# Attention and FFN in fp32r pairs: the rounding remainders of the W2 chunks moved from GpSimd to VectorE

## The chip, the cores and the metric

The kernel runs on one core of a Trainium2 chip. Its time is the device time of one execution in microseconds (us). The engines are named as the profile names them: PE is TensorE, with PEld for its weight loads, DVE is VectorE, ACT is ScalarE, POOL is GpSimd, and SP is SyncE, which issues the DMAs. Each engine works through its own instructions strictly in the order in which the program lists them, and waits for other engines at semaphores.

## The reference

For 8 batches of 8 heads, 576 positions and 64 features per head, the reference computes two attentions, one over positions pooled by four and one over a band of seven neighbours, and adds them. The heads side by side make x of 8 x 576 x 512, on which a mixing block works:

```
out_d = softmax(q_d @ k_d.T / 8) @ v_d          # q_d, k_d, v_d: means over 4 positions
attn  = repeat(out_d, 4) + local_attn(q, k, v)  # |i - j| < 4
x     = heads of attn side by side              # [8, 576, 512]
u     = x + (x.T @ U @ V).T                     # U [576, 32], V [32, 576]
out   = u + relu(u @ w_ch1) @ w_ch2             # w_ch1 [512, 2048], w_ch2 [2048, 512]
```

U, V, w_ch1 and w_ch2 arrive in float64.

## The kernel before

A pair of heads is one unit of attention work: pair 4b + hp of batch b. Pairs 0 to 4 go through a version of the attention for the start of the kernel; the pairs from 5 on go through `late_global` (pooled attention), `local_attn` (band) and `mix_part` (U and V), which leave u of the pair as two tiles, uH (rounded to fp32r) and uL (the remainder). In `late_global` PE's `ps_a` matmuls (L552) give the pooled result, DVE scales it (`od`, L556), and SP stores it with four DMAs (L561). `mix_part` loads the pair's x from DRAM (`xL`, L822), splits it (ACT L839, POOL L840), multiplies by U on PE (`ps_hu`, L848, which needs the converted `Ust`) and by V (`ps_u`, L863), and ends in uH (ACT L869) and uL (POOL L871).

The FFN runs in 256 steps, (batch, half of 288 positions, one of 16 hidden chunks of 128). Step n of `ffn1` (F1 n, twelve matmuls at L888) uses W1 chunk n mod 16 and all four pairs' u of its batch; ACT (hH, L895) and DVE (hL, L896) turn its PSUM bank into two tiles; step n of `ffn2` (F2 n, twelve matmuls at L911) uses W2 chunk n mod 16. F1 33 is the first step of batch 1 and therefore the first that needs the u of pair 7.

Each weight matrix is held as a rounded part (H) and a remainder (L), since a product is taken as H·H + H·L + L·H. `convert` makes both from a raw float64 chunk: ACT takes the absolute value (L341), four DVE instructions build the float32 bits in the tile `cT` (L342, L344, L347, L349), ACT rounds them (L351, W2H), and POOL subtracts (L354, W2L). W1 and W2 come in 16 chunks of 128 x 512 each. Raw chunks wait in three buffers which they share with the product tiles `Pt` of the local attention (L799, L804). The tile `cT` also has three buffers.

No order is written by hand: every instruction is a `Plan.op` with a duration, a priority and its dependencies, and `Plan.run` plays a list schedule with those durations and emits every engine's instructions in the order that comes out. FFN steps have the lowest priority and fill PE. A changed duration or engine thus reorders all five engines from there on.

Of the kernel before, what the change touches and what calls it, by code (L numbers as in the profile page):

```python
# [11 lines left out]
F32 = mybir.dt.float32  # L12
# [4 lines left out]
ALU = mybir.AluOpType  # L17
# [36 lines left out]
class Plan:  # L54
# [6 lines left out]
    def buf(self, pool, shape, dt, name, tag=None, bufs=1):  # L61
        return Buf(self, pool, shape, dt, name, tag or name, bufs)

    def op(self, eng, dur, fn, r=(), w=(), prio=0.0, after=(), lat=None, move=0.0, at=0.0):
        o = Op()
        o.eng, o.dur, o.fn, o.prio, o.succ, o.ndep, o.ready = eng, dur, fn, prio, [], 0, at
        o.lat, o.move = LATENCY[eng] + SLACK * (SLACK_FROM <= prio < 1000) if lat is None else lat, move
        deps = set(after)
        bufs = []
        for k in r:  # L70
            b = k[0] if isinstance(k, tuple) else k
            bufs.append(b)
            if k in self.last_w:
                deps.add(self.last_w[k])
            self.readers.setdefault(k, []).append(o)
        for k in w:
            b = k[0] if isinstance(k, tuple) else k
            bufs.append(b)
            if k in self.last_w:
                deps.add(self.last_w[k])  # L80
            deps.update(self.readers.get(k, ()))
            self.readers[k] = []
            self.last_w[k] = o
        deps.discard(o)
        o.margin = MARGIN[eng] * (MARGIN_FROM <= prio < 1000 and any(d.eng != eng for d in deps))
        o.bufs = [b for b in dict.fromkeys(bufs) if isinstance(b, Buf)]
        for b in o.bufs:
            b.uses += 1
        for d in deps:
            d.succ.append(o)  # L90
        o.ndep = len(deps)
        self.ops.append(o)
        return o
# [108 lines left out]
def attn_mix_ffn_kernel(ctx: ExitStack, tc, q, kp, vp, qT, kT, v, U, Ub, V, w1, w2, mask, band, eye, pat, pool, vw, vn, ident, outT):  # L202
    nc = tc.nc
    B, H, S, D = q.shape
# [32 lines left out]
    op, buf = plan.op, plan.buf  # L237
# [24 lines left out]
    def dve(n, fn, r, w, prio, two_x=False):  # L262
        return op(DVE, ((n / 2 if two_x else n) + 65) / 960.0, fn, r, w, prio)

    def act(n, fn, r, w, prio, base=0.143):
        return op(ACT, n / 1200.0 + base, fn, r, w, prio)

    def pool_tt(n, fn, r, w, prio, ns=2.11, after=()):
        return op(POOL, 0.147 + n * ns / 1000.0, fn, r, w, prio, after)
# [10 lines left out]
    W2 = {}  # L280
# [39 lines left out]
    for _ in range(2):  # L320
        m = kept_tile([NS, 2, KW], "ms_b")
        op(POOL, 0.4, lambda m=m: nc.gpsimd.tensor_copy(
            out=m()[:, :, :, KL:KW].rearrange("p r h k -> p (r h) k"),
# [11 lines left out]
    def convert(raw, pp, n, hi_out, lo_out, a, wkey, name, prio, gate=(), l0=0):  # L335
        t = buf(ffn, [128, CN], I32, name, "cT:" + name, 3)
        w = lambda i: raw()[:pp, :2 * n].rearrange("p (n two) -> p n two", two=2)[:, :, i]
        ti = lambda: t()[:pp, :n]
        tf = lambda: t()[:pp, :n].bitcast(F32)
        ta = lambda: tf().rearrange("p (a n) -> p a n", a=a)  # L340
        act(n, lambda: nc.scalar.activation(tf(), w(1).bitcast(F32), AF.Abs), [raw], [t], prio)  # L341
        dve(1.6 * n, lambda: nc.vector.tensor_scalar(  # L342
            out=tf(), in0=tf(), scalar1=F_MIN, scalar2=F_MAX, op0=ALU.max, op1=ALU.min), [t], [t], prio, True)
        dve(1.6 * n, lambda: nc.vector.tensor_scalar(  # L344
            out=ti(), in0=ti(), scalar1=5, scalar2=2, op0=ALU.logical_shift_left,
            op1=ALU.logical_shift_right), [t], [t], prio, True)
        dve(1.2 * n, lambda: nc.vector.scalar_tensor_tensor(  # L347
            ti(), w(1), -0x40000000, ti(), op0=ALU.bitwise_and, op1=ALU.bitwise_or), [raw, t], [t], prio)
        dve(1.2 * n, lambda: nc.vector.scalar_tensor_tensor(  # L349
            ti(), w(0), 29, ti(), op0=ALU.logical_shift_right, op1=ALU.bitwise_or), [raw, t], [t], prio)  # L350
        act(n, lambda: nc.scalar.activation(hi_out(), ta(), AF.Copy), [t, *gate], [wkey + "H"], prio)  # L351
        if lo_out is None:
            return
        pool_tt(1.0 * n, lambda: nc.gpsimd.tensor_tensor(  # L354
            out=lo_out(), in0=ta()[l0:], in1=hi_out()[l0:].bitcast(F32), op=ALU.subtract),
            [t, wkey + "H"], [wkey + "L"], prio)

    def early_raw(name):
        return buf(early_pool, [128, S], I32, name, "eraw", 1)
# [4 lines left out]
    def load_ublk(prio):  # L364
        raw = early_raw("ur")
        dma(lambda raw=raw: nc.sync.dma_start(
            out=raw()[:, :2 * NS * R], in_=Ub.bitcast(I32)), [], [raw], prio, 164)
        convert(raw, 128, NS * R, lambda: Ublk[:, :, 0:R], None, NS, "Ub", "cu", prio)

    def load_u(prio):  # L370
        raw = raw_buf("ur")
        dma(lambda raw=raw: nc.sync.dma_start(out=raw()[:MP, :2 * MJ * R], in_=U.bitcast(I32)),
            [], [raw], prio, 150)
        convert(raw, MP, MJ * R, lambda: Ust[:, :, 0:R], lambda: Ust[:, :, R:2 * R], MJ, "U", "cu", prio)

    def load_v(prio):
        hs = S // 2
        for c in range(2):
            raw = early_raw("vraw")

            dma(lambda raw=raw, c=c: nc.sync.dma_start(
                out=raw()[:, :2 * hs], in_=V.bitcast(I32)[:, c * S:(c + 1) * S]), [], [raw], prio)
            cs = slice(c * hs, (c + 1) * hs)
            convert(raw, 128, hs, lambda cs=cs: Vst[:, cs].unsqueeze(1),
                    lambda cs=cs: Vst[3 * R:4 * R, cs].unsqueeze(1), 1, f"V{c}", "cv", prio, l0=3 * R)
# [590 lines left out]
    for i in range(len(steps) + LAG):  # L976
        if i < len(steps):
            b, t, fc = steps[i]
# [72 lines left out]
```

## Time and profile before

| | |
|---|---|
| Median of 3 runs (lowest, highest) | 1037.44 us (1034.21, 1039.74) |
| The profiled execution's own time | 1038.36 us |
| Its span | 1036.60 us |
| PE, PEld busy | 996.9 us, 975.3 us |
| DVE, ACT, POOL busy | 529.8 us, 388.0 us, 557.2 us |
| W2 chunks: first and last W2L instruction start | 100.7 us, 165.1 us |

The span is the stretch that the profiler recorded; the execution's own time has 1.76 us around it. Busy times of the whole span hide stages, so the rows further down are read stage by stage.

### The profile page before, as it was taken

The page shows a single profiled execution, that of the slowest core. Times are in us where ns is not written, and L with a number is a line of the kernel's source. Part 1 is how long each engine was busy: PE and PEld are TensorE (multiplying, and loading weights), DVE is VectorE, ACT ScalarE, POOL GpSimd, SP SyncE. Part 2 cuts the span into 40 slices and gives each one's busy share as a digit, 9 for nine tenths or more (in the row PEclk, how much of TensorE's full clock was granted, in tenths as well). Part 3 has the DMA queues.
Part 4 walks back from the last instruction along what each step waited for, and adds up shares of the span by engine and source line. Part 5 has one row for each costly group of instructions (what it writes and reads, how often), then busy time and mean ns, then how long its engine had stood idle before and what let it go on. Part 6 is the DMA issues. An engine that isn't in the chain of part 4 may idle for free.

```text
span 1036.6 us, 26946 instructions
## 1 busy us (share of the span) xinstructions
PE 996.9 (96%) x10831; PEld 975.3 (94%) x10831; DVE 529.8 (51%) x1054; ACT 388.0 (37%) x1234; POOL 557.2 (54%) x567
## 2 busy tenths in 40 slices
PE   6778898999999999999999999999999999999998
PEld 5667888999999999999999999999999999999998
DVE  5997898655554545444475344534652544211111
ACT  3676554442443434443344244423443232111110
POOL 4854568788575656565585638762765625211010
PEclk9896999999999999999999999999999999999999
DMA  8866764753555545545555355624644242000000
GB/s 279 226 172 179 199 186 116 149 138 104 135 137 115 141 113 132 128 86 146 120 137 125 87 132 133 143 75 101 151 116 117 64 113 50 24 1 24 1 24 23
DMA packets 222612, 120.30 MB, mean 116 GB/s; under 512 B 175492, under 2 KB 198456, under 8 KB 222488
## 3 DMA queue, kind: packets, MB, share of 16 engines
q1 hardware_dynamic: 222488, 118.58, 45.5%
q8 instruction: 85, 1.39, 0.6%
q14 instruction: 39, 0.32, 0.1%
HBM read 87.78 MB, written 30.75 MB: 114 GB/s over the span
## 4 chain that ended last, share of the span: by engine, by line
PE 84%; DVE 7%; POOL 3%; issue 2%; DMA 2%; ACT 2%; SPq 0%; DVEq 0%; POOLq 0%; ACTq 0%
PE acc L911 36%; PE ps_h L888 35%; PE ps_a L552 2%; PE ps_b L719 2%; DVE c L347 2%; PE ps_hu L848 1%; DVE c L349 1%; PE ps_t L539 1%; DMA w2r<-in_W 1%; PE ps_b L726 1%; POOL Pt L799 1%; DVE c L342 1%; DVE c L344 1%; PE ps_a L484 1%; PE ps_v L431 1%
## 5 line engine op out<-in xcount | busy, mean ns | idle before, releaser
L911 PE MATMUL acc<-hH,W2H 128*128 128x288 f32 x1024 | 310.5, 303 | 0.0
L896 DVE SCALAR_TENSOR_TENSOR hL<-ps_h,hH 128x288 fp32r<-128x288 f32 x256 | 116.6, 455 | 378.6 <-ACT hH L895 378.0
L888 PE MATMUL ps_h<-uH,W1H 128*128 128x288 f32 x1024 | 304.3, 297 | 4.1 <-DVE hL L896 3.1
L911 PE MATMUL acc<-hH,W2L 128*128 128x288 f32 x1024 | 303.1, 296 | 2.6 <-POOL W2L L354 2.6
L888 PE MATMUL ps_h<-uL,W1H 128*128 128x288 f32 x1024 | 303.4, 296 | 1.2 <-POOL uL L871 1.2
L911 PE MATMUL acc<-hL,W2H 128*128 128x288 f32 x1024 | 302.6, 296 | 0.0
L888 PE MATMUL ps_h<-uH,W1L 128*128 128x288 f32 x1024 | 302.0, 295 | 0.0
L799 POOL TENSOR_TENSOR Pt<-vl,at 128x896 f32<-128x896 f32 (+1 forms) x135 | 233.4, 1809 | 115.1 <-DVE acc L804 61.1
L895 ACT ACTIVATE hH<-ps_h 128x288 fp32r<-128x288 f32 x256 | 105.1, 410 | 433.6 <-PE ps_h L888 433.5
L888 PEld LDWEIGHTS ps_h<-uH,W1H 128*128 128x128 f32 x1024 | 193.5, 189 | 5.4 <-DVE hL L896 3.8
L911 PEld LDWEIGHTS acc<-hH,W2L 128*128 128x128 f32 x1024 | 193.2, 189 | 3.5 <-POOL W2L L354 3.5
L888 PEld LDWEIGHTS ps_h<-uL,W1H 128*128 128x128 f32 x1024 | 193.4, 189 | 1.5 <-POOL uL L871 1.5
L911 PEld LDWEIGHTS acc<-hH,W2H 128*128 128x128 f32 x1024 | 193.3, 189 | 1.1
L888 PEld LDWEIGHTS ps_h<-uH,W1L 128*128 128x128 f32 x1024 | 193.7, 189 | 0.0
L911 PEld LDWEIGHTS acc<-hL,W2H 128*128 128x128 f32 x1024 | 193.7, 189 | 0.0
L804 DVE TENSOR_REDUCE acc<-Pt 128x128 f32<-128x1024 f32 (+1 forms) x135 | 144.7, 1103 | 4.7 <-POOL Pt L799 2.3
L871 POOL TENSOR_TENSOR uL<-xT,uH 128x288 fp32r<-128x288 f32 x56 | 44.1, 811 | 71.3 <-ACT uH L869 71.2
L921 POOL TENSOR_TENSOR o<-uH,uL 128x288 f32<-128x288 f32 x64 | 49.8, 816 | 54.2 <-DMA out_t<-o 54.2
L840 POOL TENSOR_TENSOR xL<-xL,xH 116x640 fp32r<-116x640 f32 x28 | 44.0, 1572 | 64.2 <-ACT xH L839 49.3
L510 POOL TENSOR_TENSOR vr<-vr 72x256 f32<-72x256 f32 x54 | 42.4, 785 | 46.9 <-DMA vr<-in_v 46.8
L793 ACT ACTIVATE Pt<-ul 128x128 f32<-128x128 f32 (+1 forms) x135 | 48.4, 441 | 21.3 <-DVE acc L804 20.0
L744 ACT ACTIVATE se<-ps_b 96x114 f32<-96x114 f32 x108 | 38.5, 357 | 47.1 <-PE ps_b L719 34.1
(129 smaller groups left out, 1106.9 us busy)
## 6 DMA issues: line engine op xcount, KB each, us to landing
vl<-in_vp SPq DMA_DIRECT2D x54, 240.0 KB
out_t<-o SPq DMA_DIRECT2D x64, 144.0 KB
w1r<-in_W SPq DMA_DIRECT2D x16, 512.0 KB
w2r<-in_W SPq DMA_DIRECT2D x16, 512.0 KB
Y<-x_s SPq DMA_DIRECT2D x112, 72.0 KB
gT<-in_kT SPq DMA_DIRECT2D x27, 291.0 KB
xL<-x_s SPq DMA_DIRECT2D x28, 280.0 KB
gq<-in_qT SPq DMA_DIRECT2D x27, 288.0 KB
```

Source lines behind the costliest of these rows:

```text
L510: pool_tt(256, lambda x=x: nc.gpsimd.tensor_tensor(out=x()[:, :, 0:2, :], in0=x()[:, :, 0:2, :], in1=x()[:, :, 2:4, :], op=ALU.add), [x], ...
L744: act(n * KL, lambda p=ps[hh], se=se, n=n, rows=rows: nc.scalar.activation(se()[rows, 0:n].rearrange("p r k -> p (r k)"), p()[rows, 0:n * ...
L793: act(n * D, lambda n=n, ps=ps, Pt=Pt: nc.scalar.activation(Pt()[:, :n, :, 7], ul()[:, ps, :], AF.Copy), [ul], [(Pt, 1)], prio, 0.16)
L799: nc.gpsimd.tensor_tensor(out=Pt()[:, :n, :, 0:7].rearrange("p s d o -> p o s d"), in0=win, in1=at()[:, ps, :].rearrange("p s o -> p o s") ...
L804: dve(8.5 * n * D, lambda n=n, ps=ps, Pt=Pt: nc.vector.tensor_reduce(out=acc()[:, ps, :], in_=Pt()[:, :n], axis=AX.X, op=ALU.add), [(Pt, 0 ...
L840: pool_tt(640, lambda: nc.gpsimd.tensor_tensor(out=xL(), in0=xL().bitcast(F32), in1=xH().bitcast(F32), op=ALU.subtract), [xL, xH], [xL], prio)
L871: pool_tt(TN, lambda uH=uH, uL=uL, uf=uf: nc.gpsimd.tensor_tensor(out=uL()[:, hp, :], in0=uf(), in1=uH()[:, hp, :].bitcast(F32), op=ALU.su ...
L888: nc.tensor.matmul(ps()[:, :TN], w[:, dc, fs], u()[:, dc, :], start=(n == 0), stop=(n == 3 * NDC - 1))
L895: last_h[i] = act(TN, lambda: nc.scalar.activation(hH(), ps()[:, :TN], AF.Relu), [ps], [hH], FIRST, 0.05)
L896: dve(TN, lambda: nc.vector.scalar_tensor_tensor(hL(), ps()[:, :TN], 0.0, hH().bitcast(F32), op0=ALU.max, op1=ALU.subtract), [ps, hH], [hL ...
L911: nc.tensor.matmul(ac[e]()[:, :TN], W2[w][:, fc, es], hx(), start=(fc == 0 and n == 0), stop=(fc == NFC - 1 and n == 2))
L921: pool_tt(TN, lambda e=e, o1=o1: nc.gpsimd.tensor_tensor(out=o1()[:, :TN], in0=uH()[:, e, :].bitcast(F32), in1=uL()[:, e, :].bitcast(F32), ...
```

## The change

In `convert`, the subtraction for keys that begin with "W2" goes to DVE as a `tensor_tensor` of the same operands, planned with a length of 1.1 times the chunk; those of W1, U and V stay on POOL. Nothing else in the code changes, but the plan does, from the first W2 chunk on.

```
-        pool_tt(1.0 * n, lambda: nc.gpsimd.tensor_tensor(
-            out=lo_out(), in0=ta()[l0:], in1=hi_out()[l0:].bitcast(F32), op=ALU.subtract),
-            [t, wkey + "H"], [wkey + "L"], prio)
+        on = nc.vector if wkey[:2] == "W2" else nc.gpsimd
+        put = lambda: on.tensor_tensor(out=lo_out(), in0=ta()[l0:], in1=hi_out()[l0:].bitcast(F32), op=ALU.subtract)
+        (lambda *x: dve(1.1 * n, *x) if on is nc.vector else pool_tt(1.0 * n, *x))(
+            put, [t, wkey + "H"], [wkey + "L"], prio)
```

The new code has one line more, so behind `convert` its line numbers are one higher (the subtraction itself stands at L355).

On DVE, at the second and third W2 chunk (`c_1538`, `c_1591`; a number names one buffer of `cT`), there stands before:

```order
L347 SCALAR_TENSOR_TENSOR c_1538<-w2r,c_1538 128x512
L349 SCALAR_TENSOR_TENSOR c_1538<-w2r,c_1538 128x512
L342 TENSOR_SCALAR c_1591<-c_1591 128x512
L770 SCALAR_TENSOR_TENSOR ms<-sc,mask_sb 128x63
L344 TENSOR_SCALAR c_1591<-c_1591 128x512
L772 TENSOR_REDUCE lmx<-ms 128x9
L520 TENSOR_REDUCE mx<-ps_b 72x2
L347 SCALAR_TENSOR_TENSOR c_1591<-w2r,c_1591 128x512
```

and now:

```order
L347 SCALAR_TENSOR_TENSOR c_1538<-w2r,c_1538 128x512
L355 TENSOR_TENSOR W2L<-c_1528,W2H 128x512
L349 SCALAR_TENSOR_TENSOR c_1538<-w2r,c_1538 128x512
L342 TENSOR_SCALAR c_1591<-c_1591 128x512
L771 SCALAR_TENSOR_TENSOR ms<-sc,mask_sb 128x63
L521 TENSOR_REDUCE mx<-ps_b 72x2
L355 TENSOR_TENSOR W2L<-c_1538,W2H 128x512
L344 TENSOR_SCALAR c_1591<-c_1591 128x512
L897 SCALAR_TENSOR_TENSOR hL<-ps_h,hH 128x288
L347 SCALAR_TENSOR_TENSOR c_1591<-w2r,c_1591 128x512
```

Each chunk's subtraction stands one to five instructions behind the L349 of its own chunk, with pieces of the next chunk and of the attention between them; ACT's rounding has to happen in that gap. At the narrowest place (sixth chunk) only one short instruction and one L342 stand in it.

On PE, the first `ps_hu` matmuls that need `Ust` (pair 4) stand before between F1 18 and F2 16:

```order
L888 MATMUL ps_h_2562<-uL_838,W1H_88 128x288
L888 MATMUL ps_h_2562<-uH_832,W1L_89 128x288
L848 MATMUL ps_hu_2598<-xH_1705,Ust_86 64x128 x5
L848 MATMUL ps_hu_2598<-xL_1557,Ust_86 64x128 x5
L911 MATMUL acc0_1652<-hH_2497,W2H_1567 128x288
```

and now between F1 21 and F2 17:

```order
L889 MATMUL ps_h_2643<-uL_838,W1H_88 128x288
L889 MATMUL ps_h_2643<-uH_832,W1L_89 128x288
L849 MATMUL ps_hu_2666<-xH_1689,Ust_86 64x128 x5
L849 MATMUL ps_hu_2666<-xL_1557,Ust_86 64x128 x5
L912 MATMUL acc0_2687<-hH_2493,W2H_1567 128x288
```

Between the same attention work, 48 FFN matmuls (F1 19, 20 and 21, and F2 16) have come to stand ahead of them.

Further on in PE's order, the `ps_a` matmuls of pair 9 stand before within F2 27, behind F1 29:

```order
L911 MATMUL acc2_2693<-hH_3166,W2L_1568 128x288
L552 MATMUL ps_a_3295<-vs_3034,E_2905 72x64 x4
L552 MATMUL ps_a_3295<-vs_3268,E_2920 72x64 x4
L863 MATMUL ps_u_3310<-Vst_87,stk_3275 128x288
L911 MATMUL acc3_2699<-hH_3166,W2H_1567 128x288
```

and now within F2 28, behind F1 30:

```order
L912 MATMUL acc2_2724<-hH_3195,W2L_1568 128x288
L553 MATMUL ps_a_3335<-vs_2832,E_2934 72x64 x4
L553 MATMUL ps_a_3335<-vs_3289,E_2975 72x64 x4
L912 MATMUL acc3_2703<-hH_3195,W2H_1567 128x288
```

They have moved back by 26 matmuls: one F1, one F2 and the two `ps_u` of pair 6, which both stood behind them before.

On SP, the load of the last W2 chunk stood ahead of the four `od` stores of pair 7 and of the score stores of pair 8; it now stands behind the four `od` stores and the first four of the eight score stores. The `od` stores of pair 9 stand, as before, directly ahead of the load of `xL` of pair 7. On POOL the sixteen W2L instructions are gone, and the first three `Pt` products come closer together.

## Rows read from the trace of the kernel before

**Rows 1.** The page: the span, the engines' busy times, PE's 40 slices in tenths.

```profile
span 1036.6 us, 26946 instructions
...
PE 996.9 (96%) x10831; PEld 975.3 (94%) x10831; DVE 529.8 (51%) x1054; ACT 388.0 (37%) x1234; POOL 557.2 (54%) x567
...
PE   6778898999999999999999999999999999999998
```

**Rows 2.** Busy us by stretch: PE, PEld, DVE, ACT, POOL; granted clock, DMA share, GB/s.

```profile
100.00:125.00 25.00, 22.81 (x251) 21.75 (x250) 21.32 (x39) 13.77 (x38) 12.36 (x10) 0.93 0.82 213
125.00:150.00 25.00, 23.24 (x259) 21.93 (x260) 22.82 (x40) 13.65 (x37) 16.40 (x18) 0.93 0.64 190
150.00:175.00 25.00, 20.51 (x233) 19.57 (x232) 23.89 (x41) 12.59 (x41) 20.60 (x16) 0.93 0.43 111
...
128.00:132.00 4.00, 4.00 (x109) 3.55 (x109) 3.97 (x12) 1.60 (x4) 1.18 (x2) 0.63 0.21 42
...
168.00:172.00 4.00, 3.98 (x24) 3.98 (x25) 3.32 (x11) 1.88 (x10) 4.00 (x5) 0.57 0.35 103
```

**Rows 3.** Waits of PE from 96 to 205 us: total, times, longest.

```profile
PE acc L911 <- POOL W2L L354: 2.6, 4, 1.0
PE ps_hu L848 <- POOL Ust L354: 2.5, 1, 2.5
PE ps_h L888 <- DVE hL L896: 2.3, 2, 1.4
PE ps_a L552 <- POOL vs L512: 0.5, 1, 0.5
PE ps_t L539 <- ACT E L525: 0.5, 1, 0.5
```

**Rows 4.** Timeline of DVE (start, duration, instruction), from 96 us on.

```profile
101.26 1.65 DVE L349 SCALAR_TENSOR_TENSOR c<-w2r,c 128x512 int32<-128x512 int32 x1
...
111.31 0.68 DVE L349 SCALAR_TENSOR_TENSOR c<-w2r,c 128x512 int32<-128x512 int32 x1
111.91 0.42 DVE L342 TENSOR_SCALAR c<-c 128x512 f32<-128x512 f32 x1
...
156.90 4.02 DVE L342 TENSOR_SCALAR c<-c 128x512 f32<-128x512 f32 x1
```

**Rows 5.** Timeline of POOL at the first and at the last of those DVE instructions.

```profile
100.70 1.66 POOL L354 TENSOR_TENSOR W2L<-c,W2H 128x512 fp32r<-128x512 f32 x1 [2.53 <-ACT W2H L351]
...
159.35 1.28 POOL L354 TENSOR_TENSOR W2L<-c,W2H 128x512 fp32r<-128x512 f32 x1
```

**Rows 6.** The tile W2L on POOL: durations in ns (least, median, most), first and last start.

```profile
L354 POOL TENSOR_TENSOR W2L<-c,W2H x16: 1263/1312/3420, 100.7 to 165.1; 128x512 fp32r<-128x512 f32 x16
```

**Rows 7.** Timeline of ACT at the fourth and the sixth W2 chunk.

```profile
112.03 0.63 ACT L351 ACTIVATE W2H<-c 128x512 fp32r<-128x512 f32 x1 [1.40 <-DVE c L349]
...
119.88 0.67 ACT L341 ACTIVATE c<-w2r 128x512 f32<-128x512 f32 x1 [3.62 <-DMA w2r<-in_W]
120.45 0.62 ACT L351 ACTIVATE W2H<-c 128x512 fp32r<-128x512 f32 x1
```

**Rows 8.** Timeline of PE: pair 9's `ps_a`, F1 30, pair 7's `ps_hu`, F1 33.

```profile
211.83 1.19 PE L552 MATMUL ps_a<-vs,E 72*72 72x64 f32 x16
...
213.45 0.29 PE L888 MATMUL ps_h<-uH,W1H 128*128 128x288 f32 x1
...
215.04 0.29 PE L863 MATMUL ps_u<-Vst,stk 128*128 128x288 f32 x1
...
226.01 0.47 PE L848 MATMUL ps_hu<-xH,Ust 116*64 116x128 f32 x5
...
232.06 0.40 PE L888 MATMUL ps_h<-uL,W1H 128*128 128x288 f32 x1 [1.23 <-POOL uL L871]
```

**Rows 9.** Timeline of SP's queue: pair 9's `od` stores, pair 7's `xL` load.

```profile
213.51 3.74 SPq L561 DMA_DIRECT2D up_s<-od  x4
217.36 0.47 SPq L822 DMA_DIRECT2D xL<-x_s  x1
```

## The prediction

> **What bounds the kernel now.** I read the page first. PE is busy for 996.9 of 1036.6 us, and its slices are full from the eighth on; before that they are at 5 to 8 tenths [rows 1]. So the time is PE's work plus what PE idles or runs slowly in the first 235 us, and a change that only touches DVE and POOL can move the time only through that. The windows then show where: from 100 to 175 us PE is busy for 22.81, 23.24 and 20.51 of 25 us, while DVE is the fullest of the other engines (21.32, 22.82, 23.89) [rows 2]. The W2 conversion lies just there, its sixteen subtractions on POOL starting between 100.7 and 165.1 us [rows 6]. The list of PE's waits says what ended the idle time: W2L 2.6, Ust 2.5, hL 2.3, and 0.5 twice for attention work, together 8.4 us [rows 3]. The granted clock adds to it: it stands at 0.63 from 128 to 132 us and at 0.57 from 168 to 172, where the 2.5 us wait for Ust has just ended [rows 2, 3]. These are stretches mixed from the two levels of 1.2 and 2.4 GHz, and they cost (1 - 0.63) x 4 = 1.5 and (1 - 0.57) x 4 = 1.7 us. So 8.4 + 3.2 = 11.6 us is all that this stage can give back.
>
> A second place decides whether it is given back. F1 33 needs the u of pair 7 and waits for POOL's uL until 232.06 us [rows 8]. Followed back, that chain goes over `ps_hu` of pair 7 at 226.01 to the load of its `xL` at 217.36, which SP could issue only behind the `od` stores of pair 9 (213.51, 3.74 us), and those need pair 9's `ps_a` on PE at 211.83 [rows 8, 9]. From `ps_a` to F1 33 it is 20.2 us, of which PE's place in its own order sets the start. Behind F1 33 the slices are full again. The end thus moves by as much as pair 9's `ps_a` moves.
>
> **What the change removes.** DVE's timeline shows an effect of POOL that the groups hide. L349 on a 128x512 chunk lasts 0.68 us at 111.31, but 1.65 at 101.26, and POOL runs a W2L from 100.70 until 102.36: DVE's instruction ends 0.55 us after POOL's, as if it had begun there [rows 4, 5]. Fourteen DVE instructions from 101.26 to 161 us overlap a W2L in this way. Their excess over the clear duration, counted only until the W2L ends (0.98 us for the first; for the last, the 4.02 us L342 at 156.90, the 1.1 us of the W2L at 159.35 in which no other POOL instruction ran), adds up to 13.0 us. This goes.
>
> **What it adds.** Sixteen subtractions of 128x512 with two operands from SBUF. The nearest row is L349, of the same shape and also with two tensors read: L342 starts 0.60 us behind it (111.31 to 111.91) [rows 4]. 16 x 0.60 = 9.6 us of DVE time. The Trainium skill, "VectorE: DVE Perf Modes", section "The TRN2 errata", gives a float32 tensor_tensor (N + 151) / 0.96 ns, an estimate of 0.69 us here and 11.1 us for sixteen; by it the DVE sum would be 1.5 us worse.
>
> The new subtraction can wait in two ways. It needs ACT's rounding, which needs L349: at its best ACT takes 0.63 us [rows 7] and starts at once, and the DVE work put between (one to five instructions) mostly covers that. Five of sixteen roundings came late, by 3.6 us in all, as at 120.45, where ACT stood at the load of the next chunk until 119.88 [rows 7]. I take 2 us. What stands behind it on DVE is the next chunk and an hL, and for hL PE waits. And it can meet POOL's other work: POOL is busy for 49.4 us of these 75, of which some 16 x 1.31 = 21 are W2L [rows 2, 6], so it is met a third of the time, for about half a POOL instruction, 0.45 us: 16 x 0.34 x 0.45 = 2.4 us. DVE's balance is -13.0 + 9.6 + 2 + 2.4 = +1.0; without either wait it is -3.4, with waits of a whole W2L's length (0.98) each it is +12.3. So DVE is not relieved by much and the W2 chunks come about when they came. POOL saves 21 us here, which no wait of PE asks for: it waited for ACT.
>
> **What it moves.** (1) 48 FFN matmuls now stand ahead of the first `ps_hu`. At 1.59 us for twelve (F1 30 from 213.45 to the next instruction at 215.04) [rows 8] that is 6.4 us of cover, so the 2.5 us wait for Ust goes and, with the gap, the 1.7 us of slow clock behind it: 4.2 us. F2 16 among them now needs the last W2L, whose load comes later on SP, behind stores that PE's attention work releases; I take the last chunk to be ready at about 166 us, as before (165.1 + 1.3) [rows 6]. (2) Of the waits for W2L and hL, 4.9 us, I take back 3: a chunk's remainder takes 0.6 us on DVE where it took 1.3 and more on POOL, but hL shares DVE with it. The 1.0 us for attention work and the slow clock at 128 us stay. Recovered: 7.2 of 11.6 us; the ends are 0 and 11.6. (3) Pair 9's `ps_a` stands 26 matmuls later: 26 x 1.59 / 12 = 3.4 us more work ahead of it. With all F2 steps of batch 0 now done before pair 7's `ps_hu`, less FFN work covers the way to F1 33, but the way itself is no longer.
>
> **The sum.** +3.4 - 7.2 = -3.8 us. Against the profiled execution's 1038.36 that is 1034.6; this execution lies 0.9 above the median of 1037.44, so for the median 1033.6. The ends of the recovered time give 1037.44 + 3.4 = 1040.8 and 1037.44 + 3.4 - 11.6 = 1029.2.
>
> **The rivals.** What a measurement of this kernel can tell from no change is about 0.5%, 5.2 us, so 1032.3 and 1042.6 are the borders.
> - *PE gets nearly all of it back.* If neither wait of the new subtraction is there, DVE saves 3.4 us, the chunks come ahead of PE, and 9 to 11.6 us are recovered: 1029 to 1032 for the median. For it: only one gap on DVE is shorter than ACT's rounding. Against it: DMA is at 0.82 and 0.64 of its share in the first two windows [rows 2], and ACT waited for raw chunks, so the pace of the loads may hold. 0.3.
> - *The subtraction meets POOL in full: slower.* If each of the sixteen waits about as long as L349 did behind a W2L, DVE ends the stage 12.3 us later instead of 1.0; F2 16 and all behind it start 11 us later than in the forecast, and the time is 1045. It crosses the border at 9 us instead of 11, an average wait of (10 + 13.0 - 9.6) / 16 = 0.84 us. For it: in the 4.02 us row one DVE instruction let several of POOL's pass, and three `Pt` products now stand close together near the last chunks. Against it: the long POOL instructions of this stage were the W2L themselves. The Trainium skill, "SBUF — State Buffer", section "Who interferes with whom", speaks for it: a DVE instruction with two SBUF inputs and a GpSimd instruction that reads SBUF exclude each other, and the second to issue waits in full. By that rule the move changes who waits but doesn't end the conflict. The trace agrees with the waiting (0.98 us); how often it is met no run shows yet. 0.10.
> - *Nothing changes.* What PE gets back by 170 us it stands still for at F1 33, since the loads and stores of pairs 5 to 7 set that time and not PE's order: 1037. For it: PE had 1.23 us of waiting there already [rows 8]. Against it: the chain's start is on PE. It lies within the borders, as the forecast does: 0.6 together, of which 0.45 for the forecast.
>
> Chances: faster 0.3, same 0.6, slower 0.1. The range from 1029 to 1041 holds the forecast, the unchanged case and most of the gain; it leaves out the slower rival and the deepest gain.
>
> **What would show each step.** Right: L347 and L349 on w2r mostly at 0.68 us, with few above 1.3; the W2L group on DVE has a mean of 0.7 to 0.9 us; no wait of PE for Ust, and a clock of 1.00 behind 168 us; pair 9's `ps_a` near 209 us and F1 33 near 229 us; the rest of the slices full as before. Wrong: a W2L group on DVE of more than 1.2 us, or DVE idle for ACT's W2H by more than 4 us in all; PE waits for W2L or hL above 5 us in sum; a wait at F1 33 of more than 4 us, by which PE's gain would be lost again; or PE gaps behind 240 us, which before had none and which would mean that the new order starves a later batch.

## The result, and the profile of the changed kernel

| | before | the change |
|---|---|---|
| Median, 20 runs each (lowest, highest) | 1038.32 us (1034.21, 1042.65) | 1041.99 us (1038.79, 1046.42) |
| Ratio to before, 95% interval | | 1.0037 [1.0025, 1.0050] |
| The profiled execution, its span | 1038.36, 1036.6 us [rows 1] | 1040.94, 1039.2 us |

The forecast was 1033.6 us, 3.8 faster; the change is 3.7 us slower, just above the forecast range of 1029 to 1041. The page of the changed kernel (span, busy times, PE's slices in tenths) shows PE's work unchanged and POOL relieved of 23 us:

```profile
span 1039.2 us, 26944 instructions
...
PE 994.1 (96%) x10831; PEld 972.6 (94%) x10831; DVE 531.2 (51%) x1070; ACT 387.1 (37%) x1234; POOL 534.2 (51%) x551
...
PE   6778898999999999999999999999999999999998
```

To compare stages I use one measure throughout: **PE's loss** in a stretch is the time in which it was not busy plus (1 - granted clock) x length of the stretch. The clock has two digits, so the value of one window is good to some 0.3 us. The windows of the kernel before (columns as in [rows 2]):

```profile
100.00:150.00 50.00, 46.05 (x510) 43.68 (x510) 44.14 (x79) 27.42 (x74) 28.76 (x27) 0.93 0.73 202
150.00:200.00 50.00, 45.51 (x524) 44.32 (x523) 38.97 (x69) 23.76 (x77) 38.04 (x33) 0.97 0.52 130
200.00:260.00 60.00, 58.00 (x608) 57.09 (x608) 34.16 (x64) 20.93 (x64) 50.70 (x47) 1.00 0.52 125
```

and of the changed one:

```profile
100.00:150.00 50.00, 42.44 (x490) 39.98 (x489) 41.60 (x86) 26.17 (x73) 12.85 (x16) 0.97 0.73 193
150.00:200.00 50.00, 45.53 (x534) 44.29 (x534) 40.34 (x79) 24.88 (x79) 29.53 (x26) 1.00 0.51 126
200.00:260.00 60.00, 57.48 (x541) 56.96 (x541) 36.34 (x65) 20.28 (x64) 51.09 (x47) 0.97 0.58 139
```

From 100 to 200 us, before: 3.95 + 3.5 + 4.49 + 1.5 = 13.4; now: 7.56 + 1.5 + 4.47 + 0 = 13.5. The W2 stage gave back nothing in this profile. From 200 to 260 us it is 2.0 before and 2.52 + 1.8 = 4.3 now. What ended PE's idle time from 96 to 205 us, and then from 205 to 260 us:

```profile
PE ps_h L889 <- DVE hL L897: 7.4, 6, 2.3
PE acc L912 <- ACT W2H L351: 2.3, 1, 2.3
PE acc L912 <- DVE W2L L355: 1.4, 2, 0.7
PE ps_a L553 <- ACT E L544: 0.8, 1, 0.8
PE ps_b L727 <- DVE od L557: 0.8, 1, 0.8
...
PE ps_u L864 <- DVE stk L854: 1.7, 1, 1.7
PE ps_hu L849 <- POOL xL L841: 0.8, 1, 0.8
```

The wait for Ust (2.5 us in [rows 3]) is gone and W2L has fallen from 2.6 to 1.4, but hL has risen from 2.3 to 7.4 and W2H has come with 2.3. The second place is new: PE stands at pair 7's `ps_hu` and `ps_u` instead of at F1 33 [rows 8]. The subtraction itself behaves as forecast (its tile on DVE; durations least, median, most):

```profile
L355 DVE TENSOR_TENSOR W2L<-c,W2H x16: 671/680/1123, 102.3 to 169.6; 128x512 fp32r<-128x512 f32 x16
```

### The profile page after: what moved, and what is told of

Same layout as the page of the kernel before. It is cut to its first block, busy times and chain, and to the rows that moved or that the text cites. A ratio compares the mean times of both kernels' runs of the same rounds, so it can differ in the third digit from the quotient of the medians.

```text
span 1039.2 us, 26944 instructions
## 1 busy us (share of the span) xinstructions
PE 994.1 (96%) x10831; PEld 972.6 (94%) x10831; DVE 531.2 (51%) x1070; ACT 387.1 (37%) x1234; POOL 534.2 (51%) x551
## 4 chain that ended last, share of the span: by engine, by line
PE 86%; DVE 5%; DMA 4%; ACT 2%; issue 1%; SPq 0%; DVEq 0%; ACTq 0%
PE acc L912 37%; PE ps_h L889 37%; PE ps_a L553 2%; DMA w2r<-in_W 2%; PE ps_b L720 2%; PE ps_hu L849 2%; PE ps_t L540 1%; PE ps_b L727 1%; PE ps_a L485 1%; DVE c L347 1%; PE ps_u L864 1%; DVE c L349 1%; PE ps_v L432 1%; DMA s_s<-se 1%; DVE c L342 0%
## 5 line engine op out<-in xcount | busy, mean ns | idle before, releaser
L805 DVE TENSOR_REDUCE acc<-Pt 128x128 f32<-128x1024 f32 (+1 forms) x135 | 144.7, 1103 | 6.2 <-ACT Pt L794 2.9
L745 ACT ACTIVATE se<-ps_b 96x114 f32<-96x114 f32 x108 | 38.4, 356 | 51.3 <-PE ps_b L720 38.4
```

The costliest lines, as they stand in the source:

```text
L745: act(n * KL, lambda p=ps[hh], se=se, n=n, rows=rows: nc.scalar.activation(se()[rows, 0:n].rearrange("p r k -> p (r k)"), p()[rows, 0:n * ...
L805: dve(8.5 * n * D, lambda n=n, ps=ps, Pt=Pt: nc.vector.tensor_reduce(out=acc()[:, ps, :], in_=Pt()[:, :n], axis=AX.X, op=ALU.add), [(Pt, 0 ...
```

## The experiments

Every kernel was compared with the kernel before on the same chip; the kernel before had medians of 1038.1 to 1039.3 us there, so the ratios compare, not the medians. The change ran 20 times, the others 6 to 12 times. All results, with PE's loss worked out as above from each one's own windows:

| kernel | median us | ratio [95%] | loss 100-200 | loss 200-260 |
|---|---|---|---|---|
| before (two profiles) | | | 13.4, 13.9 | 2.0, 2.6 |
| the change (two profiles) | 1041.99 | 1.0037 [1.0025, 1.0050] | 13.5, 12.7 | 4.3, 4.8 |
| e1: old order, DVE | 1037.62 | 0.9983 [0.9970, 0.9995] | 11.7 | 2.1 |
| e2: new order, POOL | 1046.98 | 1.0083 [1.0064, 1.0102] | 19.2 | 3.8 |
| e3: old order, none | 1036.51 | 0.9976 [0.9957, 0.9995] | 8.9 | 2.9 |
| e4: new order, none | 1041.12 | 1.0011 [0.9995, 1.0027] | 12.8 | 4.4 |
| e5: change, W2 loads up | 1041.55 | 1.0039 [1.0019, 1.0059] | 10.2 | 8.0 |
| e6: old order, pair 9 later | 1041.93 | 1.0028 [1.0012, 1.0044] | 14.1 | 4.7 |
| e7: change, another plan | 1044.88 | 1.0059 [1.0039, 1.0079] | 15.3 | 3.8 |
| e8: e1, W2 loads up | 1040.18 | 1.0023 [1.0005, 1.0041] | 12.9 | 2.6 |
| e9: change, pair 7 loads up | 1043.81 | 1.0045 [1.0024, 1.0066] | 14.7 | 3.4 |
| e10: e1, pair 7 loads up | 1038.12 | 1.0001 [0.9981, 1.0022] | 12.3 | 2.6 |
| e11: e5, pair 7 loads up | 1041.79 | 1.0028 [1.0013, 1.0043] | 11.5 | 7.1 |
| e12: e9, pair 7 chain up | 1042.84 | 1.0050 [1.0036, 1.0065] | 15.0 | 5.6 |
| e13: e11, pair 7 chain up (two profiles) | 1043.65 | 1.0054 [1.0041, 1.0067] | 10.9, 10.7 | 5.4, 5.6 |
| e14: e10, pair 7 chain up | 1038.99 | 1.0006 [0.9990, 1.0022] | 11.7 | 4.8 |

### The engine and the order apart (e1 to e4)

The change does two things: another engine subtracts, and the plan lists everything in another order. e1 keeps the old plan and issues the subtraction on DVE; e2 keeps the new plan and issues it on POOL; e3 and e4 leave the subtraction out under either plan, and their matmuls read W2H where they would read W2L, so their output is not the reference's.

```
e1, against before:
-        pool_tt(1.0 * n, lambda: nc.gpsimd.tensor_tensor(
+        on = nc.vector if wkey[:2] == "W2" else nc.gpsimd
+        pool_tt(1.0 * n, lambda: on.tensor_tensor(
e2, against the change:
-        put = lambda: on.tensor_tensor(...)
+        put = lambda: nc.gpsimd.tensor_tensor(...)
e3 and e4, against before and the change (where wkey[:2] == "W2", planned but nothing issued):
...
-                for n, (w, hx) in enumerate((("H", hH), ("H", hL), ("L", hH))):
+                for n, (w, hx) in enumerate((("H", hH), ("H", hL), ("H", hH))):
```

> The plan still counts the W2 subtractions as POOL's, so PE, ACT and SP have exactly the order of before; only the sixteen instructions are emitted on DVE, where the plan's start times put them. Order theory (the loss is the new order: pair 9's ps_a 26 matmuls later, the last W2 load behind score stores): no loss here, 3 to 6 us faster than before, since the 13 us of DVE stalls behind W2L go and 9.6 us come. Engine theory (sixteen subtractions in DVE's line, waiting for ACT, delay hL and W2L whatever the order): 3 to 5 us slower than before, as the change.

> The plan counts the W2 subtractions as DVE's, so PE, ACT and SP have exactly the order of the change; the sixteen instructions are emitted on POOL. Order theory: slower than before by 3 us or more, like the change, or worse by the stalls that POOL's W2L bring back. Engine theory: within 1 us of before.

> Order of before with the sixteen W2 subtractions left out and the matmuls that read W2L reading W2H instead (same number and shape). The bound of what the subtraction costs on either engine in this order. Order theory: about as e1 or 1 to 3 us better, so 4 to 9 us faster than before. Engine theory: 4 us or more faster than e1.

> Order of the change with the sixteen W2 subtractions left out, W2H read in place of W2L. Order theory: still not faster than before (1037 to 1042), since loads and the places on PE stay. Engine theory: 4 us or more faster than the change, so at or below before.

Read the ratios by columns. New against old order costs 0.0054 with DVE (5.6 us), 0.0083 with POOL (8.6 us; before itself is the old order) and 0.0035 with nothing (3.6 us). DVE in place of POOL gains 1.8 us in the old order and 4.8 in the new one. So the engine is not what makes the change slower; the order is, and it does so even where there is no subtraction at all. The order theory has the direction in all four, but not the size: e1 was to gain 3 to 6 us and e3 4 to 9. e3 is also the ceiling of what the engine can give: without any W2 subtraction the old order gains 2.5 us (interval 0.5 to 4.5), and e1 has 1.8 of them.

PE's waits say the same. In the eight profiles of the old order, with the subtraction on POOL, on DVE or left out, PE waits 1.6 to 2.6 us for Ust and 1.5 to 3.5 for hL from 96 to 205 us. In the ten profiles of the change's order (e7 has another) it never waits for Ust, and 4.7 to 7.9 us for hL; e4, without any subtraction, has the 4.7.

Why POOL is so much dearer in the new order has one visible part. In e2 PE waits 4.9 us for one hL, which stands on DVE behind a short instruction on U's chunk that lasts 3.38 us (0.23 in the change) while POOL runs three instructions one after another, the last of them a W2L that ends at 172.59. From the timelines of PE and DVE in e2:

```profile
174.24 0.61 PE L889 MATMUL ps_h<-uH,W1H 128*128 128x288 f32 x1 [4.92 <-DVE hL L897]
...
169.31 3.38 DVE L344 TENSOR_SCALAR cu<-cu 116x160 int32<-116x160 int32 x1
```

### Pair 9 moved alone (e6)

Pair 9's `ps_a`, `od` and stores, and pair 7's loads behind them, stand 24 FFN matmuls and two `ps_u` later in the old order.

```
...
+        nxt = [x for x in ffn if at[x] > at[group[0]]]
+        order = [x for x in order if x not in self.late]
+        i = order.index(nxt[LATER - 1]) + 1
+        order[i:i] = group
```

> The kernel before, with one thing moved: pair 9's ps_a, its od multiplication and store, and pair 7's xL and Y loads behind them stand 24 FFN matmuls and two ps_u later, about where the change has them. If the chain ps_a, od, store, xL load, ps_hu sets the start of F1 33, as the prediction's step (3) has it, TensorE waits 4 to 5 us more for xL or uL ahead of F1 33 and the kernel takes 3 to 4 us more than before: 1041 to 1043 us. If the chain has slack, the wait grows by under 1 us and the time is that of before within 1 us: 1038 to 1040 us, and the change's 4 us come from the W2 stage alone.

It costs 2.9 us, interval 1.2 to 4.6, and the loss from 200 to 260 us rises from 2.0 and 2.6 to 4.7. The waits grow less than expected: uL from 1.2 to 2.1 us, and 1.8 us in four short ones ahead of it (1.0 for xL). The forecast's term of +3.4 us for this move holds in size.

### The W2 loads ahead of the score stores (e5, e8)

In the change the last W2 load is issued at 158.81 us (150.62 before), behind `od` stores and the first score stores, and ACT waits 14.8 us for these loads instead of 9.0. Both kernels list each W2 load directly behind the last use of the buffer that it fills.

```
...
+                to = max([first[held[k - 1]]] + [last[b] for b in held[:k - 2]]) + 1
+                if to < at[o]:
+                    order.remove(o)
+                    order.insert(to, o)
```

> The change with one thing altered: on the SP queue the six later W2 loads stand directly behind the last use of the buffer that they replace, ahead of the score stores that they stood behind; every other engine's order is the change's. Theory L (the late W2 loads set the pace of the W2 stage: the last load was issued 8.2 us later than before and ACT waited 14.8 us for loads): 2 to 4 us faster than the change, 1038 to 1040 us, with ACT's waits for the W2 loads under 9 us, the last W2L before 168 us and TensorE's waits for hL behind 164 us under 2.5 us. Theory D (VectorE's own line, in which hL stands behind the softmax work of the next pair, sets the pace): as the change, within 1 us (1041 to 1043), TensorE's hL waits stay above 4 us. Theory S (the stores that are pushed back cost as much as the loads gain): within 1 us too, but with waits for the score tiles' buffers in place of those for hL.

> The order of the kernel before, with the W2 subtraction on VectorE and the six W2 loads ahead of the score stores on SP. Theory L: 1 to 3 us faster than before, 1035 to 1037 us, and at least 0.5 us faster than the same order without the loads moved (ratio below 0.997 to before). Theory D or S: the same as without the loads moved, ratio 0.997 to 1.000 to before.

In e5 ACT's wait for the loads falls to 8.9 us, the first `ps_hu` comes at 173.5 instead of 177.1, and the loss of the W2 stage falls from 13.5 to 10.2. The late loads thus cost part of that stage (the four profiles of the new order with the loads up lose 10.2 to 11.5 us there, the four of the change, e9 and e12 12.7 to 15.0). But it is the part ahead of 150 us: the loss falls there from 9.1 and 7.2 in the change's two profiles to 5.3, and behind it stays (4.5 and 5.5 against 4.9). The last W2L now starts at 165.9 instead of 169.6, and still PE waits 4.0 us for hL behind 164 us, where it waited 4.5; theory L asked for under 2.5, and theory D's two signs are there (the time, and 5.7 us for hL in all). And the time stays, because the loss from 200 to 260 rises from 4.3 to 8.0. This is the window, and the place in PE's timeline (start, duration, instruction, wait and its releaser):

```profile
200.00:260.00 60.00, 55.64 (x510) 54.09 (x509) 35.36 (x62) 19.83 (x62) 51.21 (x47) 0.94 0.56 129
...
227.92 0.47 PE L869 MATMUL ps_hu<-xH,Ust 116*64 116x128 f32 x5
229.19 0.52 PE L869 MATMUL ps_hu<-xL,Ust 116*64 116x128 f32 x5 [0.81 <-POOL xL L861]
231.47 0.51 PE L884 MATMUL ps_u<-Vst,stk 128*128 128x288 f32 x2 [1.76 <-DVE stk L874]
```

What PE gains by 175 us it stands still for at pair 7's chain. In the old order (e8) the same move is slower than e1, 1.0023 against 0.9983: that fits none of the three expectations, and which of the stores pushed back is missed there was not isolated.

### Pair 7's loads, then its whole chain (e9 to e14)

e9, e10 and e11 issue pair 7's `xL` and `Y` loads ahead of pair 9's `od` stores. e12, e13 and e14 also list its xH, xL, `ps_hu`, stk, `ps_u`, xT, uH and uL earlier, by 4.0 us of the plan's time (2.5 in e14).

```
e9 to e14:
...
+        i = order.index(self.stores9[0])
+        rest = [x for x in order[i:] if x not in self.seven]
+        return order[:i] + self.seven + rest
e12 to e14:
...
+        order = [(s - self.chain7.get(o, 0.0), i, o) for s, i, o in order]
         order.sort(key=lambda x: x[:2])
```

> The change with one thing altered: on the SP queue pair 7's xL and Y loads stand ahead of pair 9's od stores, behind which they waited for pair 9's ps_a (issued at 222.0 us, though the x_s that they read was stored from 214.0 us on); every other engine's order is the change's. Theory C (what the change lost lies in this chain: ps_a of pair 9, od, od stores, xL load, ps_hu of pair 7): xL is loaded some 5 us sooner, the waits for xL and stk ahead of F1 33 (0.8 and 1.7 us) and the slow clock behind them (0.83 from 230 to 240) go, and the kernel is 2 to 4 us faster than the change: 1038 to 1040 us, ratio 0.999 to 1.001. Theory W (the loss is the W2 stage's): within 1 us of the change, ratio 1.003 to 1.005. Theory X (another transfer or POOL's queue binds next): the two waits move to other tiles and the time stays.

> The order of the kernel before with the W2 subtraction on VectorE, and pair 7's xL and Y loads ahead of pair 9's od stores on SP. Theory C: the wait for uL ahead of F1 33 (1.2 us) and most of hL's behind it (0.8) go: ratio to before 0.9960 to 0.9975, 1.0 to 2.0 us under the same order without the loads moved. Theory W or X: 0.9975 to 0.9995, as without.

> The change with both SP moves: the W2 loads ahead of the score stores, and pair 7's xL and Y loads ahead of pair 9's od stores. The W2 loads alone brought the first ps_hu from 177.1 to 173.5 us, and the time did not follow. Theory C: with the chain of pair 9 out of the way the 3.6 us come through to the end, 4 to 6 us faster than the change, 1035.5 to 1037.5 us, ratio 0.9965 to 0.9990. Theory W or X: the gain is lost again ahead of 250 us, ratio above 1.0015.

In e9 the xL load is issued 1.8 us behind pair 9's `ps_a` instead of 5.5, and nothing is gained: PE still waits 0.8 us for xL and 1.8 for stk, since xL now stands late in POOL's own line. In the kernel before it stands ahead of pair 6's uL and a `Pt`, in the new order behind both. POOL's timeline before, and of e9:

```profile
223.72 1.58 POOL L840 TENSOR_TENSOR xL<-xL,xH 116x640 fp32r<-116x640 f32 x1 [1.94 <-DMA s_s<-se]
225.26 2.33 POOL L871 TENSOR_TENSOR uL<-xT,uH 128x288 fp32r<-128x288 f32 x3
```

```profile
229.43 2.33 POOL L883 TENSOR_TENSOR uL<-xT,uH 128x288 fp32r<-128x288 f32 x3 [1.86 <-ACT uH L881]
231.72 2.02 POOL L809 TENSOR_TENSOR Pt<-vl,at 128x896 f32<-128x896 f32 x1
233.58 1.55 POOL L852 TENSOR_TENSOR xL<-xL,xH 116x640 fp32r<-116x640 f32 x1
```

The path that the forecast drew from `ps_a` over `od`, store and load is thus not the binding one in the new order. That is theory X's cause, though the two waits have not moved to other tiles. e11 loses its gain ahead of 250 us, as theories W and X have it, and e10 comes out at 1.0001, above every expectation, with an interval that reaches down to W's and X's. The next three kernels take POOL's line out as well:

> The change with pair 7's chain moved up as a whole: its xL and Y loads ahead of pair 9's od stores on SP, its xH, xL, stk, xT, uH and uL work further up on ScalarE, GpSimd and VectorE, and its ps_hu ahead of the last 12 F2 matmuls in front of ps_u on TensorE, which had nothing between ps_hu and ps_u to work on. Theory C2 (the 48 FFN matmuls that the change put ahead in the W2 stage are missing as cover for this chain): the waits for xL (0.8 us) and stk (1.7 us) and the slow clock behind them (1.7 us) go, and the kernel is 2 to 4 us faster than the change: ratio to before 0.9995 to 1.0020. Theory W (the change lost its time in the W2 stage): ratio 1.0030 to 1.0050, as the change. Theory X (the next wait, for uL or hL behind ps_u, takes what is gained): the same ratio, with waits of 2 us and more for uL or hL ahead of 245 us.

> The change with pair 7's chain moved up and the W2 loads ahead of the score stores. The loads alone brought the first ps_hu forward by 3.6 us, which was lost again ahead of 250 us. Theory C2: with the chain up the 3 us come through, 4 to 6 us faster than the change, ratio to before 0.9965 to 1.0000. Theory X: the gain is lost again, ratio above 1.0015, with waits for uL or hL behind ps_u. Theory W: 1 to 2 us faster than the change, from the loads alone.

> The order of the kernel before with the W2 subtraction on VectorE and pair 7's chain moved up as a whole (loads, xH, xL, ps_hu, stk, ps_u, xT, uH, uL). Theory C2: TensorE's waits for uL (1.2 us) and hL (0.8 us) behind pair 7's ps_u go, ratio to before 0.9955 to 0.9980, some 1 to 2 us under the same order without the move (0.9983). Theory X: the wait moves to another tile and the ratio is 0.998 to 1.000.

Theory X again in e12 and e13; e14 lies at 1.0006, just above it. The waits for xL and stk go, and a wait for hL behind F1 33 takes their place: 2.7 us in e12 and e13, and 2.5 in e14, where the old order had 0.8. From PE's timeline in e13's second profile, where `ps_hu` and `ps_u` now wait for next to nothing, and from DVE's:

```profile
226.29 0.52 PE L881 MATMUL ps_hu<-xH,Ust 116*64 116x128 f32 x5 [0.34 <-ACT E L571]
...
228.61 0.43 PE L896 MATMUL ps_u<-Vst,stk 128*128 128x288 f32 x2
...
230.99 0.40 PE L923 MATMUL ps_h<-uL,W1H 128*128 128x288 f32 x1 [0.47 <-POOL uL L904]
...
235.84 0.61 PE L923 MATMUL ps_h<-uH,W1H 128*128 128x288 f32 x1 [2.74 <-DVE hL L931]
236.25 0.44 PE L923 MATMUL ps_h<-uL,W1H 128*128 128x288 f32 x1
236.49 0.44 PE L923 MATMUL ps_h<-uH,W1L 128*128 128x288 f32 x1
```

```profile
233.61 1.81 DVE L834 TENSOR_REDUCE acc<-Pt 128x128 f32<-128x1024 f32 x2 [1.05 <-POOL Pt L829]
235.34 0.45 DVE L931 SCALAR_TENSOR_TENSOR hL<-ps_h,hH 128x288 fp32r<-128x288 f32 x1
```

ACT had the hH for that hL ready at 232.04; DVE came to hL only behind two reductions of the local attention, which waited for POOL's `Pt`. By then every F2 step of batch 0 is done, so nothing stands between F1 steps to cover that. Behind the wait the matmuls start 0.24 us apart instead of 0.13: the slow clock costs a further 1.8 us in that window.

### Another plan (e7)

The planner counts 1.0 instead of 1.1 ns an element; no instruction differs, only the order.

```
-        (lambda *x: dve(1.1 * n, *x) if on is nc.vector else pool_tt(1.0 * n, *x))(
+        (lambda *x: dve(1.0 * n, *x) if on is nc.vector else pool_tt(1.0 * n, *x))(
```

> The change, but the planner counts 1.0 ns an element for the subtraction on VectorE in place of 1.1: 512 counted as 512 and not 563 ns, no instruction and no engine differs, only the order that the planner makes. Theory O (each list order has its own time, and the change's was an unlucky one among several): another order gives another time, 1034 to 1040 us, at least 2 us from the change. Theory P (an order that is planned with the subtraction on VectorE is slower for a reason that they share: W2 chunks later and the FFN put ahead of them): within 1.5 us of the change, 1040.5 to 1043.5 us.

The ratio is 0.0022 (2.3 us) above the change's, but the intervals overlap, so whether a 10% smaller number in the plan gives another time is not shown. It lies above the ranges of both theories. Its waits lie elsewhere, though: hL has 0.2 us, W2L 3.9 and W2H 3.4. Both orders planned for DVE are slower than the old one; two are too few to say that they must be.

### Second profiles (before, the change, e13)

Nothing is edited.

> The kernel before once more, nothing altered, for a second profile. Up to the last ps_a ahead of the W2 stage all orders on TensorE are the same, and yet it started between 95.2 and 101.8 us in sixteen profiles (96.4 in the first one of this kernel). Theory R (the first 100 us are chance, with TensorE's clock at one level or the other): it starts 1 us or more from 96.4, and the rest of the span behind it is within 2 us of the first profile's 940.2. Theory K (each kernel has its own start): 96.0 to 96.8 again.

> The change once more, nothing altered, for a second profile. In the first one the last ps_a ahead of the W2 stage started at 97.8 and 941.4 us followed, 1.2 more than before, where the medians differ by 3.7. Theory R: the start differs by 1 us or more from 97.8, and the rest is 942 to 946, that is, the profile was one of the change's better ones in the W2 stage. Theory K: 97.4 to 98.2 and 941 to 942 again, so that a part of the loss lies ahead of the W2 stage.

> The change with the W2 loads and pair 7's chain up, once more. Its first profile had the last ps_a ahead of the W2 stage at 101.8, the latest of all, and only 940.7 us behind it, as before; its median is 1043.65. Theory R: the start comes at 95 to 100 us, and 942 to 946 us follow. Theory K: 101 to 102.5 again, and 940 to 942 behind: then the moves did give the time back behind 100 us, and it is lost ahead of it.

They took 1039.39, 1040.83 and 1040.22 us; one more execution of the kernel before, beside them on the same chip, took 1044.59. The `ps_a` in question, in e13's first and second profile:

```profile
101.78 1.25 PE L580 MATMUL ps_a<-vs,E 72*72 72x64 f32 x16 [0.79 <-ACT E L571]
...
95.36 1.94 PE L580 MATMUL ps_a<-vs,E 72*72 72x64 f32 x14 [0.40 <-ACT E L571]
```

One kernel, 6.4 us apart: theory R holds for e13. Before came at 96.39 and 95.33, 1.1 apart, with 2.1 us more behind it, just over R's 2; the change came at 97.79 and 96.92, 0.9 apart, between R and K, with 942.2 us behind it, as R has it. Over all profiles the mean start is 97.6 us in the eight of the old order and 97.6 in the eleven planned for DVE, so the order has no part in it. A single span therefore says little about a difference of 4 us, and the table reads stages behind 100 us.

## Why the prediction was wrong

**What bounds the kernel.** Right as far as the profiles go: from 260 to 1000 us PE idles for at most 0.5 us in any of them, and up to 97 us PE's order is the same in all. The four profiled executions of before and the change differ by 2.0 us on average (1040.94 and 1040.83 against 1038.36 and 1039.39), and the losses from 100 to 260 by 1.7 (16.0 against 17.7, the means of the table). These four stand for 2.0 of the 3.7 us between the medians; the other 1.7 are not located, and the scatter of the first 97 us is as large.

**DVE.** Right, and better than forecast. The other four instructions on the sixteen chunks take 51.9 and 51.3 us in the two profiles of before, 37.3 and 35.3 in the change and 37.4 in e1, so 14 to 16 us went where 13.0 were forecast; the sixteen subtractions take 12.0. DVE was relieved, and in the new order PE got nothing for it. The mean subtraction is 0.75 us (the median 0.68), within the forecast 0.7 to 0.9, and DVE waits 1.2 us for W2H where 2 were allowed. The 2.4 us for meeting POOL's other work were too many (by the forecast's own rows the share is (49.4 - 21) / 75 = 0.38 and not 0.34, so 2.7): four of the sixteen are longer than 0.7 us, by 0.3, 0.4, 0.2 and 0.2 us. The Trainium skill ("SBUF — State Buffer", section "Who interferes with whom") says that a DVE instruction with two inputs in SBUF contends with a GpSimd instruction that reads SBUF, and that the order of issue decides which of them is blocked. The trace agrees: in both pairs below POOL started first, and DVE ended behind it. Two of the four with the POOL instruction that they met, from the timelines of DVE and POOL:

```profile
126.11 0.94 DVE L355 TENSOR_TENSOR W2L<-c,W2H 128x512 fp32r<-128x512 f32 x1
...
165.45 0.91 DVE L355 TENSOR_TENSOR W2L<-c,W2H 128x512 fp32r<-128x512 f32 x1
```

```profile
125.98 0.52 POOL L513 TENSOR_TENSOR vs<-vr 72x128 f32<-72x128 f32 x1
...
165.20 0.61 POOL L418 TENSOR_TENSOR smq<-gh 128x144 f32<-128x144 f32 x1
```

POOL ends at 126.50 and 165.81, DVE at 127.05 and 166.36: 0.55 us later both times, as in [rows 4, 5]. The waiting of the slower rival was thus real, but it came four times and for 1.1 us in all, not sixteen times for 0.84 and more: the kernel became slower, but not by that mechanism (e1 is faster than before).

**The step that failed: "Recovered: 7.2 of 11.6 us".** The W2 stage lost 13.4 and 13.9 us before and 13.5 and 12.7 in the change: 0.5 recovered, no more than two profiles of one kernel differ. Both of its terms were priced at the wait that goes, not at what the work moved ahead then waits for. (1) The 48 matmuls do cover Ust, and the granted clock from 168 to 172 us is 1.00 instead of 0.57. But each of the three F1 among them waits for an hL, since hL empties the PSUM bank that the F1 fills (the code gives `ps_h` two). From the change's timelines of PE and DVE:

```profile
165.08 0.40 PE L889 MATMUL ps_h<-uH,W1H 128*128 128x288 f32 x1 [0.99 <-DVE hL L897]
169.69 0.40 PE L889 MATMUL ps_h<-uH,W1H 128*128 128x288 f32 x1 [1.18 <-DVE hL L897]
175.43 0.40 PE L889 MATMUL ps_h<-uH,W1H 128*128 128x288 f32 x1 [2.31 <-DVE hL L897]
```

```profile
164.17 0.49 DVE L342 TENSOR_SCALAR c<-c 128x512 f32<-128x512 f32 x1 [1.76 <-ACT c L341]
...
170.31 1.98 DVE L347 SCALAR_TENSOR_TENSOR cu<-ur,cu 116x160 int32<-116x160 int32 x1
172.20 1.21 DVE L805 TENSOR_REDUCE acc<-Pt 128x128 f32<-128x1024 f32 x1
...
174.93 0.44 DVE L897 SCALAR_TENSOR_TENSOR hL<-ps_h,hH 128x288 fp32r<-128x288 f32 x1
```

That is 4.5 us, more than the 4.2 that the term was to give. The first hL stands behind the L342 of the last chunk, for which DVE stood idle for 1.76 us; the last (F1 21's) behind a 1.98 us L347 and two L805 of 1.2. The forecast took the last chunk "to be ready at about 166 us, as before". Its load had moved on SP by 8.2 us, and its W2L ended at 170.4 us; the forecast named the move and put no price on it. F2 16 itself did not wait for that W2L, and in e5, where it is early again, 4.0 of the 4.5 us stay, so most of this wait is DVE's line and not the load. (2) Of the waits for W2L and hL 3 us were to come back; they rose from 4.9 to 8.8, above the 5 us that the forecast named as a sign of being wrong, and W2H added 2.3. e5 shows what the loads have in the stage: hoisting them recovers 2.5 to 3.3 us, all of it ahead of 150 us.

**Pair 9's `ps_a`: +3.4 us.** Right in size (e6: 2.9; the losses from 200 to 260: +2.3), wrong in the way. With nothing recovered ahead of it, `ps_a` came at 216.5 us and not near 209, and the matmul of F1 33 that needs pair 7's uL at 236.1 and not near 229. The path over the store and the load does not bind (e9, e10, e11): [rows 8] already show pair 7's `ps_hu` without a wait, and only F1 33, behind `ps_u`, with one. The forecast saw that "less FFN work covers the way to F1 33" and priced it at nothing. In the kernel before, twelve F2 matmuls stand between pair 7's `ps_hu` and `ps_u` and six behind them; in the change all eighteen are done before, PE stands still for 0.8 and 1.7 us there, and the granted clock behind that is 0.83 from 230 to 240 us, where before it was 1.00. That the missing cover is the cause is read from these rows and not shown by a run: e12 and e13 put twelve of the eighteen back between `ps_hu` and `ps_u`, and a wait for hL took the place of the two that went.

**The rivals.** "Nothing changes" had half of the better mechanism: "What PE gets back by 170 us it stands still for at F1 33". Its reason, the loads and stores, does not hold (e9 to e11), and the time did change. e5, e11 and e13 show the first half: they lose 10.2, 11.5 and 10.8 instead of 13.1 in the W2 stage, and 8.0, 7.1 and 5.5 instead of 4.5 behind it. "PE gets nearly all of it back" falls with e3 and e4: even no subtraction at all gives 2.5 us in the old order, and no gain is seen in the new one (1.0011).

**What stays open.** In e13 both profiles lose less than the change (16.3 against 17.7 us), yet the six timed runs are slower (1042.47 to 1045.39), with the separate execution on another chip, 1040.22, below all of them. Which of the instructions in DVE's and POOL's lines would have to move for hL to come in time was not tried, and of what the new order costs more with POOL (e2) only the one wait above is known.

**A better kernel.** e1 beats both: 0.9983 of before, and 0.0054 under the change. The gain is small (0.5 to 3.1 us), and it needs the old order kept.

## What to carry to other kernels

When a planner sets the order, a one-line change is two changes: run the new engine in the old order and the old engine in the new one before crediting either. Leave the instruction out once, to see the ceiling (here 2.5 us in the old order) before summing up waits. And work that is moved ahead to cover one wait has to be priced at both ends: what it waits for where it now stands, and the next wait that it no longer covers.

## What the runs showed of the hardware

The order on TensorE is the same in all kernels up to about 97 us, and the start of the same `ps_a` there varied from 95.2 to 101.8 us. Already at 14 us five equal transposes took 1.33 us in the kernel before, and 0.77 in its second profile and in e12, while the recorded clock is 1.00 in all of these stretches (the lines are of the first profile of before and of e12):

```profile
14.53 1.33 PE L643 MATMUL ps_bt<-ident_sb,ms_b 128*128 128x128 f32 x5
```

```profile
13.88 0.77 PE L654 MATMUL ps_bt<-ident_sb,ms_b 128*128 128x128 f32 x5
```

So the recorded clock does not show every slow stretch in the first 20 us, and PE counts as busy there.
